# Exponentials behind a group's third copy, bf16 size matmuls, and paired weight-block copies in a two-layer attention and SwiGLU kernel

## The chip, the cores and the metric

The kernel runs on one core of a Trainium2 chip. The metric is the device time of one execution in microseconds, taken as the median of several runs. The core's engines work side by side, each through its own queue in order: TensorE (PE, matmuls, with its weight loads shown apart as PEld), VectorE (DVE), ScalarE (ACT), GpSimd (POOL), and SyncE (SP), which issues most transfers. They wait for one another through semaphores.

## The reference

The input x has 2048 tokens of 1024 features. Two equal layers follow one another; each is an attention step and a gated feed-forward step, both with a residual and a layer norm in front:

```
x = x + A_ref(layernorm(x), wqkv, wo)        # 32 heads of 32; a token sees itself and 7 earlier tokens, 2 apart
x = x + B_ref(layernorm(x), w1, w3, w2)      # (silu(x @ w1) * (x @ w3)) @ w2, with 3584 hidden features
```

Attention has only eight logits per token and head, so it isn't a matmul: the products q·k and the weighted sum over v are elementwise work. Both layers use the same weights.

## The kernel before, in words

**Units.** The tokens are cut into four chunks of 512. A unit is one chunk of one layer's feed-forward step, eight in all; units 0 to 7 are walked in order by `b_stage`. Ahead of them `q_part` computes q, k and v for layer 0; those of layer 1 follow some units later, chunk by chunk.

**Plain and seven-product matmuls.** Units 0 and 1 compute w1, w3 and w2 as plain matmuls in `b_stage` (L1279, L1288, L1310). At the same time they prepare units 2 to 7, which use a Strassen-like form (Winograd's): a matrix product cut into 2 x 2 blocks is made of seven half-size products P1 to P7 instead of eight. For this the weight blocks are needed with certain sums and differences of theirs, in fp16. `weight_size` measures a group's weights: ACT squares them into `size` (L878), a matmul with a matrix of ones adds over the partitions (L892), and DVE makes a power of two from the sum (`scale_of`). `weight_sums` copies four blocks of the group, scaled, into one of two buffers `blocks` (ACT, L910), `differences` makes four more on DVE, in part over the copied ones (L923), and POOL's queue stores seven blocks to `t_d` in memory. `sums_of_w2` does the same for w2 (L1009, L1015, stored to `t2_d`). The two buffers are used in turn, and a buffer is free again when its store has landed.

**A group.** A group is four column blocks of w1 (m = 0, the gate) or of w3 (m = 1, up); w1 and w3 alternate, and a unit has 14 groups in two splits of 8 and 6. I number them 0 to 83 over units 2 to 7. `pipeline` interleaves each group with the one before it; PE's order is P1(i), P7(i-1), P5(i), P3(i-1), P6(i), P4(i-1), P2(i), with eight 256-column matmuls each (L1052). Four results are gathered in three PSUM banks A, B and D, with three copies by ACT:

- after P1 the first copy (L1064) puts A into B, so that P2 can add to B while P6 adds to A;
- after P5 the second copy (L1069) puts D into the buffer `s5`;
- after P6 the third copy (L1073) puts A into the buffer `su`; DVE adds it to D (L1076), for P3, and P7 goes on adding to A.

After P7 DVE makes A plus `s5` (L1088, L1090), and P4 goes on in A. `consume` takes each result on: Silu on ACT for a gate (L1227), a scaled copy on ACT (L1232) and a product on DVE (L1236) for up. There are six PSUM banks for this (two more for other work), and a bank is given again in the order in which banks came free. The down projection with w2 (`W` inside `products`, L1165, copies L1173, L1181, L1185) has the same seven products, for two row blocks each.

**Attention in between.** Attention is worked off in halves of a chunk (256 tokens), 16 in all. `score_steps` multiplies q by k on DVE and folds (L590, L510 to L514), PE adds up the heads (`gather_heads`, L604), DVE takes the maximum and subtracts it (L625, L628), ACT takes the exponential (L629), DVE sums, inverts and scales (L634 to L637), POOL's queue spreads the result (L644); `value_steps` then multiplies by v (L665). The exponential and Silu need different ACT tables, so an exponential between two gates brings two table loads. When the values of a half are there, `o_tile` runs two output tiles of it on PE (L771).

**What sets the order.** The program writes every engine's order out by hand. A planner keeps an expected time for each engine in `now` and a due time for each step. `background` gives DVE the next step of several queues that fits before a time; `act_background` does so for ACT; `between` takes output tiles whose values are expected to be there. The exponential is emitted inside the DVE step that subtracts the maximum (`exps`, L627 to L630), wherever that step falls. Each step has a cost in microseconds (0.61 for a block copy, 0.40 for a difference), and changing a cost or a number of steps changes where other work is placed.

Of the kernel before, what the change touches and what calls it, by code (L numbers as in the profile page):

```python
# [7 lines left out]
FP32 = mybir.dt.float32  # L8
BF16 = mybir.dt.bfloat16
FP16 = mybir.dt.float16  # L10
I32 = mybir.dt.int32
ALU = mybir.AluOpType
# [5 lines left out]
def kernel(  # L18
# [13 lines left out]
    nc = tc.nc  # L32
# [176 lines left out]
    tight = big[:, 6144:7168].bitcast(BF16).rearrange("p (i a t) -> p i a t", i=2, a=2)  # L209
    blocks = [big[:, 3584 * i:3584 * (i + 1)].rearrange("p (b k c) -> p b k c", b=7, k=KT // 2) for i in range(2)]  # L210
    NG = NF // FG
    ones = const.tile([P, P], FP32, name="ones")
    nc.gpsimd.memset(ones[:], 1.0)
    size = const.tile([P, 2, NG, 2], FP32, name="size")
    up_scale = const.tile([P, 2, NG], FP32, name="up_scale")
# [353 lines left out]
    def pe_requests(limit=1, must=False):  # L569

        act_background()
        while pe_queue and limit and (must or pe_queue[0][0]() + 3.5 <= now["pe"]):
            pe_queue.pop(0)[1]()
            limit -= 1

    def score_steps():

        V = nc.vector
        for g, (l, h) in enumerate(halves):
# [46 lines left out]

            def exps():  # L627
                V.tensor_tensor(L[:], L[:], mx[:].unsqueeze(1).to_broadcast([P, W, BLK]), op=ALU.subtract)  # L628
                nc.scalar.activation(E[:], L[:], ACTF.Exp, scale=scale)  # L629
                at["E"] = act(0.65, now["dve"] + 0.1, "exp")  # L630

            yield 0.70, 0.0, exps
            yield 0.0, at["E"] if "E" in at else 0.0, lambda: None
            yield 0.66, at["E"], lambda: V.tensor_reduce(sm_[:], E[:].rearrange("p w e -> p e w"), op=ALU.add,  # L634
                                                         axis=AX.X)
            yield 0.56, 0.0, lambda: V.reciprocal(rs[:], sm_[:])
# [42 lines left out]
    for u in range(len(units)):  # L679
        for f0, f1 in fsplits:  # L680
            if u >= TU:
                groups = [(m, g0 // FG) for g0 in range(f0, f1, FG) for m in range(2)]
                for i, (m, g) in enumerate(groups):
                    seq += [("early", m, g)] + ([("late", *groups[i - 1])] if i else [])
                seq += [("late", *groups[-1])]
            for g0 in range(f0, f1, FG) if u < TU else ():
                seq += [(kind, g0, min(FG, f1 - g0), (u, g0 // FG) if m == u else None)
                        for m, kind in enumerate(("w1", "w3"))]
            nq = (f1 - f0) // 2
            if u >= TU:  # L690
                seq += [("t2", fsplits.index((f0, f1)), b, nq) for b in range(7)]
            else:
                seq += [("w2", g0, nq, hh) for hh in range(2) for g0 in (f0, f0 + nq)]
        if 1 <= u and u + 3 < len(units):
            seq += [("qkv", which, h) for which in range(3) for h in range(2)]
# [176 lines left out]
    def weight_size(m, g, w, at, got):  # L872

        w_ = w[:].rearrange("p k c -> p (k c)")
        half = w_.shape[1] // 2
        up, down = up_scale[:, m, g:g + 1], down_scale[:, m, g:g + 1]
        for i in range(2):
            yield 1.95, at, lambda: nc.scalar.activation(junk, w_[:, i * half:(i + 1) * half], ACTF.Square,  # L878
                                                         accum_out=size[:, m, g, i:i + 1])

        def scale_item(ps, r):
            def emit():
                opened[0] -= 1
                nc.vector.tensor_reduce(down, ps[:], op=ALU.add, axis=AX.X)
                scale_of(down, up, down)
                got["at"] = now["dve"] + 0.1
            yield 1.0, r, emit

        def add_up(t):
            ps = side_tile([P, 2], FP32, name="size", tag="sd")  # L890
            opened[0] += 1
            nc.tensor.matmul(ps[:], lhsT=ones[:], rhs=size[:, m, g, :], start=True, stop=True)  # L892
            makes.insert(0, [scale_item(ps, pe(1, t)), None])

        t = now["act"] + 2.5
        pe_queue.append((lambda: t, lambda: add_up(t)))

    def weight_sums(m, g, w, got):

        while "at" not in got:  # L900
            yield "blocked"
        KQ = KT // 2
        for a in range(2):
            while pending[a]:
                yield "blocked"
            pending[a] += 1
            b = blocks[a]
            for i, (kh, fh) in ((0, (0, 0)), (1, (0, 1)), (3, (1, 0)), (5, (1, 1))):
                c0 = fh * 256 + a * P
                yield 0.61, max(got["at"], stored[a]), lambda: nc.scalar.activation(  # L910
                    b[:, i], w[:, kh * KQ:(kh + 1) * KQ, c0:c0 + P], ACTF.Copy,
                    scale=up_scale[:, m, g:g + 1])
            makes.append([differences(m, g, a, now["act"] + 0.1), None])
        made.add((m, g))

    pending, stored, made, held = [0] * 2, [0.0] * 2, set(), []
    junk = hsum[:].bitcast(BF16).rearrange("p k t -> p (k t)")

    def differences(m, g, a, r):

        b = blocks[a]
        for out, x, y in ((4, 5, 1), (1, 1, 0), (2, 4, 0), (6, 3, 2)):
            yield 0.40, r, lambda: nc.vector.tensor_tensor(  # L923
                b[:, out], b[:, x], b[:, y], op=ALU.add if (x, y) == (4, 0) else ALU.subtract)
        pending[a] -= 1
        nc.gpsimd.dma_start(t_d[m][g][:, 4 * a:4 * (a + 1)], b[:, 0:4])
        nc.gpsimd.dma_start(t_d[m][g][:, 8 + 3 * a:8 + 3 * (a + 1)], b[:, 4:7])
        stored[a] = now["dve"] + 7.0
# [49 lines left out]
    def total_scale(sizes_, up, down, got):  # L978
# [11 lines left out]
        def add_up(t):  # L990
            ps = side_tile([P, n], FP32, name="size", tag="sd")
            opened[0] += 1
            nc.tensor.matmul(ps[:], lhsT=ones[:], rhs=sizes_[:], start=True, stop=True)
            makes.insert(0, [scale_item(ps, pe(1, t)), None])

        t = now["act"] + 2.5
# [4 lines left out]
    def sums_of_w2(i, f, ws, loaded):  # L1001
# [3 lines left out]
        a = min((i for i in range(2) if not pending[i]), key=lambda i: stored[i])  # L1005
        pending[a] += 1
        b = big[:, a * 3584:(a + 1) * 3584].rearrange("p (b c) -> p b c", b=7)
        for j, (fh, hh) in ((0, (0, 0)), (2, (0, 1)), (1, (1, 0)), (5, (1, 1))):
            yield 0.61, max(loaded, stored[a], got2["at"]), lambda: nc.scalar.activation(b[:, j], ws[hh][fh][:, f, :], ACTF.Copy,  # L1009
                                                                             scale=up2[:])  # L1010
        r = now["act"] + 0.1

        def rest():
            for out, x, y in ((4, 5, 2), (2, 2, 0), (3, 4, 0), (6, 1, 3)):
                yield 0.40, r, lambda: nc.vector.tensor_tensor(  # L1015
                b[:, out], b[:, x], b[:, y], op=ALU.add if (x, y) == (4, 0) else ALU.subtract)
            pending[a] -= 1
            nc.gpsimd.dma_start(t2_d[i][:, :, f, :], b)
            stored[a] = now["dve"] + 7.0
# [15 lines left out]
    def pipeline(key, groups, consume, done, last, fill=None):  # L1035

        xnT = xnTs[key]
        KQ = KT // 2
        sides = dict(P1=(0, xnT[:, 0:KQ, 0:HT]), P5=(1, sums[:, 0]), P6=(2, sums[:, 1]), P2=(3, xnT[:, KQ:KT, 0:HT]),
                     P7=(0, xnT[:, 0:KQ, HT:CH]), P3=(1, sums[:, 2]), P4=(2, xnT[:, KQ:KT, HT:CH]))  # L1040

        def acc():
            return psum.tile([P, 2, HT], FP32, name="st", tag="mm")
# [12 lines left out]
        def head_part(i, name):  # L1056
# [14 lines left out]
            elif name == "P6":  # L1071
                r = run(G, name, G["A"], False, G["tB"])
                nc.scalar.copy(su, G["A"][:])  # L1073
                G["tU"] = t = act(0.5, r)
                background(t + 0.8)
                nc.vector.tensor_tensor(G["D"][:], G["D"][:], su, op=ALU.add)  # L1076
                G["tD"] = dve(0.68, max(t, G["t5"])) + 0.1
# [21 lines left out]
                consume(G, 2, G["A"][:], r)  # L1099

        n = len(groups)
        for i in range(n + 1):
            for name, tail in (("P1", "P7"), ("P5", "P3"), ("P6", "P4"), ("P2", None)):
                if i < n:
                    head_part(i, name)
# [307 lines left out]
```

## Time and profile before

| what | value |
|---|---|
| median of 3 runs | 1531.82 us (1531.68 to 1533.64) |
| the profiled execution | 1532.7 us |
| its span, first to last instruction | 1531.0 us |
| PE busy | 1518.1 us (99%) |
| DVE busy | 1201.8 us (78%) |
| ACT busy | 884.1 us (58%) |
| POOL busy | 153.7 us (10%) |
| granted TensorE clock | 1.00 |

Times inside the profile count from the start of the span. In a line of the timeline the first number is the start, the second the length, then engine, line of the program, operation, output and inputs by the program's names, and in brackets how long the engine had been idle and who released it. In the view of waits a line names who waited, for whom, the microseconds in total, how often, and the longest. Table loads are a line of their own.

### The profile page before, as it was taken

Reading aid. Unit: us, or ns where it says so; the run is one execution under the profiler, and the core shown is the slowest. Engines: PE = TensorE matmul, PEld = TensorE weight load, DVE = VectorE, ACT = ScalarE, POOL = GpSimd, SP = SyncE. Lnnn points to the kernel's source line nnn. Section 1 sums busy time; section 2 is a strip of 40 time slices with the busy share of each in tenths; the row PEclk is TensorE's granted clock in tenths of the full one; section 3 lists DMA queues with packets and bytes.
Section 4 is the critical chain, followed back from the end, with each engine's and each line's share of the span. In section 5 each row is a group of like instructions: output and inputs, shape, how many; then the busy total and the mean of one; then the engine's idle time right before and its main releaser. Section 6 shows DMA issues by size and latency. Waiting matters only on the chain.

```text
span 1531.0 us, 25095 instructions
## 1 busy us (share of the span) xinstructions
PE 1518.1 (99%) x9594; PEld 989.5 (65%) x9634; DVE 1201.8 (78%) x2126; ACT 884.1 (58%) x1388; POOL 153.7 (10%) x308
## 2 busy tenths in 40 slices
PE   9999999999999999999999999999999999999999
PEld 7666644444444577575786767766677767686865
DVE  4688998889989898989698958898678986435445
ACT  3885476567665357455565564756557445554643
POOL 1210102121211101001011010100111000000000
PEclk9999999999999999999999999999999999999999
DMA  9777969798997888979779997898969988878885
GB/s 321 202 218 215 253 226 330 272 304 289 306 320 247 280 316 294 347 264 303 263 269 324 346 268 282 280 323 302 323 225 333 338 296 282 306 272 334 318 294 203
DMA packets 261432, 439.56 MB, mean 287 GB/s; under 512 B 73856, under 2 KB 201088, under 8 KB 245056
## 3 DMA queue, kind: packets, MB, share of 16 engines
q1 hardware_dynamic: 248464, 390.90, 76.8%
q0 software_dynamic: 12704, 46.93, 8.6%
q8 instruction: 75, 1.23, 0.3%
q14 instruction: 45, 0.37, 0.1%
q10 hardware_dynamic: 144, 0.13, 0.0%
HBM read 345.90 MB, written 67.90 MB: 270 GB/s over the span
## 4 chain that ended last, share of the span: by engine, by line
PE 97%; ACT 1%; issue 1%; DVE 0%; DMA 0%; SPq 0%; ACTq 0%
PE st L1052 32%; PE ps L836 21%; PE w L1165 16%; PE po L771 7%; PE pg L1279 6%; PE pu L1288 6%; PE acc L1310 6%; PE pq L444 1%; PE L L604 0%; DMA wqkv<-in_A_wqkv_dram 0%; ACT L629 0%; ACT L1227 0%; ACT E L629 0%; ACT sg L1227 0%; DVE x_sb L1150 0%
## 5 line engine op out<-in xcount | busy, mean ns | idle before, releaser
L836 PE MATMUL ps<-xnT,wqkv 128*128 128x512 f16 (+1 forms) x1469 | 320.4, 379 | 0.2
L1052 PEld LDWEIGHTS <-early 128*128 128x128 f16 x2688 | 262.6, 98 | 40.4 <-issue 3.5
L836 PEld LDWEIGHTS <-wqkv 128*128 128x128 bf16 x1472 | 210.6, 144 | 108.1 <-issue 2.2
L1165 PE MATMUL w<-t,hT 128*128 128x512 f16 x1008 | 226.0, 379 | 0.6 <-ACT big L1185 0.5
L1052 PEld LDWEIGHTS <-late 128*128 128x128 f16 x2016 | 197.2, 98 | 30.6 <-issue 2.5
L590 DVE TENSOR_TENSOR tree<-qT,kT 128x2048 bf16<-128x2048 bf16 x128 | 156.3, 1221 | 35.8 <-DMA kT<-qkv_d 18.2
L1052 PE MATMUL st<-xnT,late 128*128 128x256 f16 x1344 | 174.2, 273 | 2.2 <-ACT big L1073 2.2
L510 DVE TENSOR_TENSOR tree<-tree 128x1024 bf16<-128x1024 bf16 x256 | 175.6, 686 | 0.9
L1052 PE MATMUL st<-big,early 128*128 128x256 f16 x1344 | 172.3, 273 | 1.6 <-ACT sg L1227 1.1
L1165 PEld LDWEIGHTS <-hT 128*128 128x128 f16 x1008 | 98.2, 98 | 112.9 <-DVE hT L1136 2.0
L1052 PE MATMUL st<-xnT,early 128*128 128x256 f16 x1344 | 165.7, 273 | 0.0
L665 DVE TENSOR_TENSOR tree<-At,vT 128x2048 bf16<-128x2048 bf16 x128 | 156.2, 1221 | 11.9 <-DMA At<-E 10.7
L1064 ACT COPY st<-st 128x512 f32<-128x512 f32 x84 | 48.3, 575 | 128.1 <-PE st L1052 127.4
L771 PE MATMUL po<-wo,oT 128*128 128x512 bf16 x486 | 110.8, 379 | 1.3
L840 ACT CAST hT<-ps 128x512 bf16<-128x512 f32 x96 | 55.8, 585 | 90.6 <-PE ps L836 88.3
L1288 PE MATMUL pu<-xnT,w3t 128*128 128x512 f16 x448 | 105.8, 379 | 0.0
L1279 PE MATMUL pg<-xnT,w1t 128*128 128x512 f16 x448 | 105.8, 379 | 0.0
L1310 PE MATMUL acc<-w2t,hT 128*128 128x512 bf16 x437 | 97.8, 379 | 0.6
L1076 DVE TENSOR_TENSOR st<-st,big 128x512 f32<-128x512 f32 x84 | 58.4, 695 | 46.9 <-ACT big L1073 46.8
L1227 ACT ACTIVATE sg<-st,down_scale 128x512 bf16<-128x512 f32 x126 | 86.6, 687 | 11.6 <-PE st L1052 11.0
L1052 PE MATMUL st<-big,late 128*128 128x256 f16 x672 | 87.1, 273 | 0.0
L771 PEld LDWEIGHTS <-oT 128*128 128x128 bf16 x512 | 50.1, 98 | 55.7
(167 smaller groups left out, 1916.6 us busy)
## 6 DMA issues: line engine op xcount, KB each, us to landing
early<-t_d SPq DMA_DIRECT2D x84, 1024.0 KB, 6.9
late<-t_d SPq DMA_DIRECT2D x84, 768.0 KB, 6.2
t<-t_d SPq DMA_DIRECT2D x42, 1024.0 KB, 7.3
t<-t_d SPq DMA_DIRECT2D x42, 768.0 KB, 5.3
wqkv<-in_A_wqkv_dram SPq DMA_DIRECT2D x28, 1024.0 KB, 8.1
w1t<-in_B_w_dram SPq DMA_DIRECT2D x14, 1024.0 KB, 7.6
w3t<-in_B_w_dram SPq DMA_DIRECT2D x14, 1024.0 KB, 11.0
t_d<-big POOLq DMA_DIRECT2D x28, 512.0 KB, 6.2
```

Of the source, the lines that this page charges most:

```text
L510: nc.vector.tensor_tensor(b, b, buf[:, 4:8, :], op=ALU.add)
L590: V.tensor_tensor(pr, qT[:], kT[:, :, k0:k0 + TCH], op=ALU.mult)
L665: V.tensor_tensor(tm.rearrange("p w (a e) -> p w a e", a=4), At[:].rearrange("p a w e -> p w a e"), win, op=ALU.mult)
L771: nc.tensor.matmul(ps[:], lhsT=oT[:, t, j * P:(j + 1) * P], rhs=wo[:, t, hh * 512:(hh + 1) * 512], start=(t == 0), stop=(t == KT - 1))
L836: nc.tensor.matmul(ps[:], lhsT=ws[kk // KH][:, kk % KH, t::KT], rhs=xnT[:, kk, :], start=(kk == 0), stop=(kk == KT - 1))
L1052: nc.tensor.matmul(out[:, a, :], lhsT=w[:, a, blk, k, :], rhs=rhs[:, k, :], start=start and a == 0 and k == 0, stop=k == KQ - 1, skip_grou ...
L1076: nc.vector.tensor_tensor(G["D"][:], G["D"][:], su, op=ALU.add)
L1165: nc.tensor.matmul(out[:], lhsT=lhs[:, k, j * P:(j + 1) * P], rhs=w[:, k, :], start=start and k == 0, stop=k == nq - 1, skip_group_check=True)
L1227: nc.scalar.activation(sg[:], src, ACTF.Silu, scale=inv)
L1279: nc.tensor.matmul(pg[:], lhsT=w1t[:, kk, fi * P:(fi + 1) * P], rhs=xnT[:, kk, :], start=(kk == 0), stop=(kk == KT - 1))
L1288: nc.tensor.matmul(pu[:], lhsT=w3t[:, kk, fi * P:(fi + 1) * P], rhs=xnT[:, kk, :], start=(kk == 0), stop=(kk == KT - 1))
L1310: nc.tensor.matmul(acc[:], lhsT=hT[:, f, j * P:(j + 1) * P], rhs=tiles[hh][f // nq][:, f % nq, :], start=(f == 0), stop=(f == f1 - f0 - 1))
```

## The change

It has three parts, and a fourth that comes with them.

First, exponentials. `exps` still subtracts the maximum on DVE, but inside `pipeline` (the flag `staged`) it appends the exponential to the list `later` instead of emitting it. `run_later`, called in P6 right after the third copy, emits the first of the list if its input is expected by then. At the end of a pipeline, what is left is emitted at once. `score_steps` is blocked until its exponential has been emitted.

Second, the size matmuls. The matrix `ones` becomes bf16, and the sizes are read as the upper halves of their fp32 words.

Third, block order. The seven blocks of a buffer stand in another order, so that two copies are one ACT instruction (planned at 1.20) and two of the four differences one DVE instruction (`diff_steps`, 0.66 + 0.42 + 0.42); w2's copies stay single, its differences are paired too. Fourth, the table `sides` and the order in which t2 blocks are loaded name the new places.

```
-    ones = const.tile([P, P], FP32, name="ones")
+    ones = const.tile([P, P], BF16, name="ones")
...
+    later, staged = [], [False]
+    def run_later():
+        if later and later[0][0] <= now["act"] + 0.5:
+            later.pop(0)[1]()
...
             def exps():
                 V.tensor_tensor(L[:], L[:], mx[:].unsqueeze(1).to_broadcast([P, W, BLK]), op=ALU.subtract)
-                nc.scalar.activation(E[:], L[:], ACTF.Exp, scale=scale)
-                at["E"] = act(0.65, now["dve"] + 0.1, "exp")
+                ready = now["dve"] + 0.1
+                def exp_():
+                    nc.scalar.activation(E[:], L[:], ACTF.Exp, scale=scale)
+                    at["E"] = act(0.65, ready, "exp")
+                if staged[0]:
+                    later.append((ready, exp_))
+                else:
+                    exp_()
             yield 0.70, 0.0, exps
-            yield 0.0, at["E"] if "E" in at else 0.0, lambda: None
+            while "E" not in at:
+                yield "blocked"
+            yield 0.0, at["E"], lambda: None
...
-                seq += [("t2", fsplits.index((f0, f1)), b, nq) for b in range(7)]
+                seq += [("t2", fsplits.index((f0, f1)), b, nq) for b in (0, 2, 1, 3, 4, 6, 5)]
...
-            nc.tensor.matmul(ps[:], lhsT=ones[:], rhs=size[:, m, g, :], start=True, stop=True)
+            nc.tensor.matmul(ps[:], lhsT=ones[:], rhs=size[:, m, g, :].bitcast(BF16)[:, 1::2], start=True, stop=True)
...
-            for i, (kh, fh) in ((0, (0, 0)), (1, (0, 1)), (3, (1, 0)), (5, (1, 1))):
+            for i, j, fh in ((0, 2, 0), (3, 6, 1)):
                 c0 = fh * 256 + a * P
-                yield 0.61, max(got["at"], stored[a]), lambda: nc.scalar.activation(
-                    b[:, i], w[:, kh * KQ:(kh + 1) * KQ, c0:c0 + P], ACTF.Copy,
+                yield 1.20, max(got["at"], stored[a]), lambda: nc.scalar.activation(
+                    b[:, i:j + 1:j - i], w[:, :, c0:c0 + P].rearrange("p (h k) c -> p h k c", h=2), ACTF.Copy,
                     scale=up_scale[:, m, g:g + 1])
...
+    def diff_steps(b):
+        tt = nc.vector.tensor_tensor
+        yield 0.66, lambda: tt(b[:, 1:5:3], b[:, 3:7:3], b[:, 0:4:3], op=ALU.subtract)
+        yield 0.42, lambda: tt(b[:, 3], b[:, 4], b[:, 0], op=ALU.add)
+        yield 0.42, lambda: tt(b[:, 5], b[:, 2], b[:, 3], op=ALU.subtract)
...
-        for out, x, y in ((4, 5, 1), (1, 1, 0), (2, 4, 0), (6, 3, 2)):
-            yield 0.40, r, lambda: nc.vector.tensor_tensor(
-                b[:, out], b[:, x], b[:, y], op=ALU.add if (x, y) == (4, 0) else ALU.subtract)
+        for step in diff_steps(b):
+            yield step[0], r, step[1]
...
-            nc.tensor.matmul(ps[:], lhsT=ones[:], rhs=sizes_[:], start=True, stop=True)
+            nc.tensor.matmul(ps[:], lhsT=ones[:], rhs=sizes_[:].bitcast(BF16)[:, 1::2], start=True, stop=True)
...
-        for j, (fh, hh) in ((0, (0, 0)), (2, (0, 1)), (1, (1, 0)), (5, (1, 1))):
+        for j, (fh, hh) in ((0, (0, 0)), (3, (0, 1)), (2, (1, 0)), (6, (1, 1))):
...
-            for out, x, y in ((4, 5, 2), (2, 2, 0), (3, 4, 0), (6, 1, 3)):
-                yield 0.40, r, lambda: nc.vector.tensor_tensor(
-                b[:, out], b[:, x], b[:, y], op=ALU.add if (x, y) == (4, 0) else ALU.subtract)
+            for step in diff_steps(b):
+                yield step[0], r, step[1]
...
-        sides = dict(P1=(0, xnT[:, 0:KQ, 0:HT]), P5=(1, sums[:, 0]), P6=(2, sums[:, 1]), P2=(3, xnT[:, KQ:KT, 0:HT]),
-                     P7=(0, xnT[:, 0:KQ, HT:CH]), P3=(1, sums[:, 2]), P4=(2, xnT[:, KQ:KT, HT:CH]))
+        sides = dict(P1=(0, xnT[:, 0:KQ, 0:HT]), P5=(1, sums[:, 0]), P6=(3, sums[:, 1]), P2=(2, xnT[:, KQ:KT, 0:HT]),
+                     P7=(0, xnT[:, 0:KQ, HT:CH]), P3=(2, sums[:, 2]), P4=(1, xnT[:, KQ:KT, HT:CH]))
...
                 nc.scalar.copy(su, G["A"][:])
                 G["tU"] = t = act(0.5, r)
+                run_later()
                 background(t + 0.8)
...
+        staged[0] = True
         for i in range(n + 1):
+            if i == n:
+                staged[0] = False
+                while later:
+                    later.pop(0)[1]()
```

## The prediction

> **What bounds the kernel now.** I read the page's busy times and its chain first, then PE's own waits, then the timeline around each of them.
>
> ```profile
> PE 1518.1 (99%) x9594; PEld 989.5 (65%) x9634; DVE 1201.8 (78%) x2126; ACT 884.1 (58%) x1388; POOL 153.7 (10%) x308
> PE 97%; ACT 1%; issue 1%; DVE 0%; DMA 0%; SPq 0%; ACTq 0%
> ```
>
> TensorE sets the end from first to last. Only two things can shorten the run: less work on PE, or fewer moments in which PE waits. PE's waits are few:
>
> ```profile
> PE st L1052 <- ACT big L1073: 2.2, 1, 2.2
> PE st L1052 <- ACT sg L1227: 1.1, 1, 1.1
> PE w L1165 <- ACT big L1185: 0.5, 1, 0.5
> PE st L1052 <- ACT st L1064: 0.4, 1, 0.4
> ```
>
> The view counts from the drawn end of a matmul, and a 256-column one is drawn 273 ns long though the next starts 109 ns later. So I take as a stall what a start is later than the start before it plus 8 x 0.109 = 0.873 us for a product (0.216 us for each 512-column matmul). The waits become 2.36 us at 989.79, 1.25 at 669.13, 0.64 at 1066.02, 0.57 at 1234.06, and 0.29 at 1159.90, too short for the view: 5.11 us. All five have an exponential just before them on ACT. The one at 1234, ACT first and then PE:
>
> ```profile
> 1228.45 0.59 ACT L1073 COPY big<-st 128x512 f32<-128x512 f32 x1 [0.62 <-PE st L1052]
> 1229.06 1.28 ACT L629 ACT_TABLE_LOAD   x1
> 1230.35 0.60 ACT L629 ACTIVATE E<-L 128x512 bf16<-128x512 f32 x1
> 1230.84 0.68 ACT L1232 ACTIVATE big<-st,down_scale 128x512 bf16<-128x512 f32 x1
> 1231.54 1.28 ACT L1227 ACT_TABLE_LOAD   x1
> 1232.84 0.69 ACT L1227 ACTIVATE sg<-st,down_scale 128x512 bf16<-128x512 f32 x1
> 1233.42 0.59 ACT L1064 COPY st<-st 128x512 f32<-128x512 f32 x1
> ...
> 1232.62 1.03 PE L1052 MATMUL st<-big,late 128*128 128x256 f16 x8
> 1234.06 1.03 PE L1052 MATMUL st<-big,early 128*128 128x256 f16 x8 [0.41 <-ACT st L1064]
> ```
>
> P6 of a group accumulates into A, so it waits until the next group's first copy (L1064) has read A. From the third copy of one group to the first of the next PE has six products, 5.24 us. ACT has, start to start, 0.61 + 1.29 + 0.49 + 0.70 + 1.30 + 0.58 and the copy's 0.59, 5.56 us, and began 0.2 us after P6 ended: 0.57 us late. The largest stall has the exponential ahead of the third copy instead, which P7 needs after only three more products:
>
> ```profile
> 984.19 1.28 ACT L629 ACT_TABLE_LOAD   x1
> ...
> 989.16 0.58 ACT L1073 COPY big<-st 128x512 f32<-128x512 f32 x1
> ...
> 989.79 1.03 PE L1052 MATMUL st<-xnT,late 128*128 128x256 f16 x8 [2.19 <-ACT big L1073]
> ```
>
> The size matmuls:
>
> ```profile
> L892 PE MATMUL size<-size,ones x28: 167/210/252, 206.4 to 476.1; 128*128 128x2 f32 x28
> 311.38 1.50 PEld L1279 LDWEIGHTS <-w1t 128*128 128x128 bf16 x8
> 311.49 1.89 PE L1279 MATMUL pg<-xnT,w1t 128*128 128x512 f16 x8
> 15.68 3.74 PE L444 MATMUL pq<-xnT,wqkv 128*128 128x128 bf16 x64
> ```
>
> Fourteen of two columns and one of sixteen, each two matmul records. From the size matmul's first start (311.35) to the next start (311.49) PE loses 0.14 us in 14 cases and 0.21 in the one that a gather follows: 2.17 us. The last line is bf16 with a new weight tile every 128 columns: (3.74 - 0.22) / 63 = 0.056 us from start to start, the weight load included.
>
> **What the Trainium skill says.** "ScalarE: Activation LUTs", section "What ACT_TABLE_LOAD costs": about 1283 ns for every table, and an ACTIVATE with one pointer operand takes about 280 + 0.833 N ns, of which 93 overlap with the next. The trace agrees: 1283 ns, and a 512-wide block copy (L910) takes 711 ns, 0.612 us from start to start. "TensorE: Matmul & The Clock Gate", section "Wait — 56ns, not 53.3ns?": 55.6 and 215.7 ns for 128 and 512 columns; here 56 and 216. "FP8 and Floating Point Precision", section "TensorE Precision Notes": true FP32 takes four passes; the trace shows two records per size matmul, so I use the measured 0.14 us. "VectorE: DVE Perf Modes", section "The perf-mode tier table": tensor_tensor has a double rate for bf16 and none above; the 2048-wide row at 1221 ns is that rate.
>
> **The exponentials.** There are 16. Seven belong to the first stages, where a late gate only delays one of six PSUM banks: with two banks of 1.73 us per step a bank comes round after 10.4 us, against 1.29 + 0.60 + 1.29 us for an exponential plus one 1.04 us copy. They cost PE nothing before or after. The other nine, in order of time, with PE's stall before and after:
>
> At 587.95 it stood ahead of a third copy and cost 0, because an attention-output tile (3.45 us of PE, from 588.59) followed. It now stands right behind the third copy of group 4, in the sequence copy, table, exponential, up, table, gate, first copy, which is that of 1228.45, and in the new order no tile follows: 0.57. At 666.49, behind the third copy of an up group, the gate activation of P4 came after both tables and P5 waited for its bank: 1.25. It moves one group on, to the sequence above: 0.57. At 985.48: 2.36. It moves behind the third copy of group 34, again the same sequence; two Square passes ahead make that copy start about 0.14 us late (0.2 + 0.485 + 2 x 1.045 + 0.48 + 0.575 = 3.83 after P1, against 3.69): 0.71. At 1064.89, in the down projection: 0.64, same order after. At 1155.70: 0.29, then the same sequence, 0.57. At 1230.35: 0.57; it moves to the last group before the down projection, where P4's gate ends about 4.6 us after P6 and the bank is wanted after 4.8 us (P4, P2, P7, six matmuls, P3): 0. The other three stand among projection copies, or ahead of the s5 copies of a down projection, with over a microsecond to spare: 0. Sums: 5.11 before, 0.57 + 0.57 + 0.71 + 0.64 + 0.57 = 3.06 after; gain 2.05. DVE doesn't wait meanwhile: its sum over E is held back until the exponential is issued.
>
> **Smaller stalls.** In two down projections (878.50, 1251.06) a 1.14 us attention product between two adds held the second third copy, 0.19 + 0.11 us. In the new order a 0.33 us fold, or nothing, stands there: gain 0.3. An apply pass ahead of a third copy cost 0.16 us in group 63; one now stands so in group 21: even.
>
> **Size matmuls.** 2.17 - 15 x 0.056 - 0.09 for the entry into the gather = 1.24 us. If the next weight load isn't hidden at all (0.11 us, from 311.38 to 311.49) it is 0.45. There is one more weight load instruction each, on a PE that loads during the matmul before. I take 1.24.
>
> **Block copies and differences.** ACT: 112 copies x 0.612 = 68.5 us become 56 x 1.04 (280 + 853 - 93 ns) = 58.2. DVE: per block 4 x 0.342 become 0.602 (the pitch of 1024 elements, L510) + 2 x 0.342, over 42 blocks 3.4 us less. Both count nothing on PE, which waits for neither there. What they do is let the planner place other work earlier: attention-output tiles of the third half come at 283.4 instead of 294.3, tables and w1/w3 loads shift by a group. Loads are issued 17 to 33 us ahead of use and land in 8 to 11; the POOL stores are as many as before. If the cover were gone, each microsecond that attention values are late is one on PE. For the third half the margin is 0.2 to 1.2 us: from the seventh of eight down-projection adds on DVE has 2.0 us left, the tile is wanted 3.45 us after that sum, and the add began 1.2 us after it before (281.65 against 280.4), at best 0.2. Margins before were 1.6 to 7.6 us. The new order of the t2 blocks only names the same blocks anew.
>
> **Sum.** 2.05 + 0.3 + 1.24 = 3.6 us. The span of 1531.0 becomes 1527.4, the profiled 1532.7 becomes 1529.1. The profiled run is 0.9 us above the median of 1531.82, so the median becomes 1528.2, 0.23% less. About 0.2%, 3.1 us, is what a measurement can tell from no change; the forecast lies just past it.
>
> **Rivals.** First, no visible change: the exponential's wait is only moved. For it: four places inherit the 0.57 us that is measured at 1234, one of which had none; with one or two more stalls of 0.6 and the exposed weight load, the gain is 3.6 - 0.8 - 0.8 = 2.0: 1529.8. Second, slower: attention values late in the first two units. The double difference reads and writes with a gap; at single rate it would take about 1.2 us against 0.66 planned, 0.54 x 42 = 23 us more on a DVE that idles 43.7 us of the 418.7 from 155.4 to 574.1, and tiles would wait: about 3.4, 7 and 7.6 us over for the third to fifth half, less margins of 2 to 4, some 10 in all: 1538. It decides from 3.6 us of waits on; a milder form is a plan that runs 2 us late at three tiles, 1534. Against: inner runs are whole 512-element rows, and L590, whose eight runs of 256 are gapped too, keeps 1221 ns for 2048. Third, better: third copies start before the planner thinks and most of the 3.06 us goes as well: 1525.5.
>
> **Chances.** Forecast 0.5, no visible change 0.31, slower 0.12, better 0.07. The forecast's own range is 1527.2 to 1529.0, which crosses the 0.2% line at 1528.76, so I count a tenth of it (0.05) as no change: faster 0.45 + 0.07 = 0.52, same 0.31 + 0.05 = 0.36, slower 0.12. The range from 1526.3 to 1532.0 leaves out most of the slower case and of the better one.
>
> **What would show it.** Right: the size matmul once, and about 0.06 us to the next start; PE's waits with L1073 and the gate gone, and four or five of about 0.6 us for first copies, 5.2 us behind a third copy with an exponential; DVE's double difference near 690 ns; the double block copy near 1.13 us. Wrong: PE waiting for oT, a double difference near 1.2 us, or a third copy behind an exponential still.

## The result and the profile after

The changed kernel takes 1552.43 us (median of 4 runs, 1550.77 to 1554.37) against 1531.82 us (1531.68 to 1533.64): 1.0132 times the time before, 95% interval 1.0115 to 1.0150. The prediction was 1528.2 us, in a range from 1526.3 to 1532.0. It had the wrong sign. The profiled execution took 1551.6 us, its span is 1549.7 us (1531.0 before).

These are the busy times of the changed kernel and the shares of its chain by engine, from its page:

```profile
PE 1525.7 (98%) x9619; PEld 986.9 (64%) x9619; DVE 1198.2 (77%) x2084; ACT 874.1 (56%) x1332; POOL 162.5 (10%) x308
PE 53%; DVE 11%; DMA 5%; ACT 4%; issue 2%; POOL 0%; ACTq 0%; DVEq 0%; SPq 0%; POOLq 0%
```

ACT is 10 us less busy and DVE 3.6 us, as forecast, but the chain is on PE for 53% of the span where it was 97%: it now runs through DVE and transfers. PE's waits from 180 to 620 us, which hold the first two feed-forward units (columns as in the view of waits before: total, times, longest):

```profile
PE po L788 <- DVE down_scale L901: 4.4, 3, 2.6
PE ps L853 <- DMA wqkv<-in_A_wqkv_dram: 3.8, 1, 3.8
PE pu L1316 <- DMA w3t<-in_B_w_dram: 2.8, 1, 2.8
PE st L1074 <- DVE st L1099: 1.8, 1, 1.8
PE ps L853 <- DVE peak L1051: 1.4, 1, 1.4
```

None of the five was there before. From start to start the stalls in this stretch are 0.49 us at 214.3, 2.81 at 286.9, 1.60 at 387.4, 2.95 at 467.1, 1.59 at 524.3, 3.96 at 529.2, 1.92 at 580.0, and 0.94, 0.38, 0.28 and 0.18 elsewhere: 17.1 us, an exponential's stall apart that comes below. Behind three of them (286.9, 467.1, 529.2) the next matmuls of 512 columns start up to 0.427 us apart in place of 0.216, some eight each time: 1.46 + 1.68 + 1.52 = 4.7 us more. Together 21.8 us, where the kernel before lost 0.2. The difference is 21.6 us. Less the 1.75 us of the size matmuls and 1.2 us gained in the first stages (the first w1 matmul starts at 191.3 against 192.5), with the stalls after 620 us, that exponential's included, nearly unchanged in sum (5.7 us against 5.9), that leaves 18.7 us, which is the difference of the spans.

What the change was to do to single instructions, it did. The groups of a pair copy, the double difference and the size matmul, of the changed kernel:

```profile
L927 ACT ACTIVATE big<-w3t,up_scale 128x1024 f16<-128x1024 bf16 x28 | 31.1, 1141 | 19.2 <-DMA t_d<-big 15.5 <-DVE up_scale L887 3.7
L939 DVE TENSOR_TENSOR big<-big 128x1024 f16<-128x1024 f16 x42 | 28.8, 686 | 20.2 <-ACT big L927 10.7 <-ACT big L1032 9.5
L909 PE MATMUL size<-size,ones 128*128 128x2 bf16 x14 | 2.3, 167 | 0.0
```

The double copy takes 1141 ns (1.13 us were forecast), the double difference 686 ns (690). A size matmul is one record, and the next matmul starts 28 ns after it (282.34 and 282.37 in the next view). What has changed beside the lengths is the end of the L939 line: DVE stood 20.2 us before a difference and waited for ACT's copies, where the kernel before had 12.8 (6.3 for w1's and w3's, 6.5 for w2's).

The largest stall behind a DVE instruction, at 287 us, as the timeline of the changed kernel shows it (start, length, instruction, idle time before it and its releaser):

```profile
279.06 0.92 POOL L1040 DMA_DIRECT2D t_d<-big  x1 [11.36 <-DVE big L941]
...
282.34 0.17 PE L909 MATMUL size<-size,ones 128*128 128x2 bf16 x1
282.37 1.89 PE L788 MATMUL po<-wo,oT 128*128 128x512 bf16 x8
283.03 0.68 DVE L1352 TENSOR_TENSOR x_sb<-x_sb,acc 128x512 bf16<-128x512 bf16 x1
283.50 5.14 ACT L1032 ACTIVATE big<-w2t,up 128x512 f16<-128x512 bf16 x8 [6.41 <-DMA t_d<-big]
286.08 0.69 DVE L939 TENSOR_TENSOR big<-big 128x1024 f16<-128x1024 f16 x1 [2.38 <-ACT big L1032]
286.69 0.15 DVE L901 TENSOR_REDUCE down_scale<-size 128x1 f32<-128x2 f32 x1
...
286.90 3.78 PE L788 MATMUL po<-wo,oT 128*128 128x512 bf16 x10 [2.65 <-DVE down_scale L901]
```

ACT's copies into a block buffer wait until the store of its former content has landed. DVE's queue has the difference of those copies next, and behind it the small reduction that reads the size matmul's PSUM bank. The attention-output tile of PE needs that bank. So one late store holds ACT, DVE and PE in turn. It went out late: from its issue to ACT's start are 4.4 us, less than the 7 us that the planner allows. That ACT waits for stores is not new (37.0 us in all before, 42.5 now, summed from the lines of the copies); what stands behind these waits is. The values of the tile (oT) had been there since 282.0, as forecast.

### The profile page after: what moved, and what is told of

Read it like the earlier page. It is cut to its first block, busy times and chain, and to the rows that moved or that the text cites. A ratio compares the mean times of both kernels' runs of the same rounds, so it can differ in the third digit from the quotient of the medians.

```text
span 1549.7 us, 24962 instructions
## 1 busy us (share of the span) xinstructions
PE 1525.7 (98%) x9619; PEld 986.9 (64%) x9619; DVE 1198.2 (77%) x2084; ACT 874.1 (56%) x1332; POOL 162.5 (10%) x308
## 4 chain that ended last, share of the span: by engine, by line
PE 53%; DVE 11%; DMA 5%; ACT 4%; issue 2%; POOL 0%; ACTq 0%; DVEq 0%; SPq 0%; POOLq 0%
PE st L1074 27%; PE w L1193 15%; PE ps L853 7%; PE po L788 5%; DMA t_d<-big 3%; DVE tree L682 2%; DVE tree L510 2%; DVE tree L597 1%; DMA xnT<-xn 1%; DMA w3t<-in_B_w_dram 1%; DVE tree L512 1%; ACT sg L1255 1%; DMA kT<-qkv_d 1%; DVE hT L1320 1%; DVE big L939 1%
## 5 line engine op out<-in xcount | busy, mean ns | idle before, releaser
L788 PE MATMUL po<-wo,oT 128*128 128x512 bf16 x512 | 117.7, 382 | 5.2 <-DVE down_scale L901 4.4
```

The source lines that it names most:

```text
L788: nc.tensor.matmul(ps[:], lhsT=oT[:, t, j * P:(j + 1) * P], rhs=wo[:, t, hh * 512:(hh + 1) * 512], start=(t == 0), stop=(t == KT - 1))
```

## The experiments

Times are medians; the kernel before ran beside each group on the same chip (1532.85 us for e3 to e6, 1533.17 for e7 to e10, 1532.44 for e1, e2, e11 and e12, 1532.40 for e13, 1532.65 for e14 to e17). Times of different groups can be compared to about a microsecond, since the kernel before differs by up to that.

### Which part of the change

e3_blocks has only the pair copies, the paired differences and the new block order. e4_exps_size has only the other two parts, e1_exps only the exponentials, e2_size only the size matmuls. e5_old_costs has the whole change, but the planner is told the old steps:

```
# e5_old_costs
-                yield 1.20, max(...), lambda: nc.scalar.activation(b[:, i:j + 1:j - i], ...)
+                yield 0.61, max(...), lambda: None
+                yield 0.61, max(...), lambda: nc.scalar.activation(b[:, i:j + 1:j - i], ...)
...
-        yield 0.66, lambda: tt(b[:, 1:5:3], b[:, 3:7:3], b[:, 0:4:3], op=ALU.subtract)
-        yield 0.42, ...   (twice)
+        yield 0.40, lambda: None
+        yield 0.40, lambda: tt(b[:, 1:5:3], b[:, 3:7:3], b[:, 0:4:3], op=ALU.subtract)
+        yield 0.40, ...   (twice)
```

e6_new_plan_single is its mirror: planned as the changed kernel, but each pair is issued as two single instructions.

```
# e6_new_plan_single
-                yield 1.20, max(...), lambda: nc.scalar.activation(b[:, i:j + 1:j - i], ...)
+                yield 1.20, max(...), lambda: [nc.scalar.activation(b[:, q], w[:, kh * KQ:...], ...)
+                                               for kh, q in enumerate((i, j))]
```

> The kernel before with the block part of the change alone (paired copies and differences, new block order, new planned costs); exponentials and size matmuls as before. If the blocks make the loss (theory), it is as slow as the changed kernel without what the other two parts gain: 1552.4 + 1.7 (size) + 0 to 2 (exponentials), 1552 to 1557. If the delayed exponentials make it (rival), 1532 within 2.

> The kernel before with the exponentials and the bf16 size matmuls alone; blocks, their instructions and their planned costs as before. Theory (blocks make the loss): 1531.8 - 1.7 (15 size matmuls at 0.028 instead of 0.145 us) - 2.05 (exponential stalls 5.11 to 3.06), 1528.0, at most 1 us off. Rival (exponentials make the loss): about 1550.

> The whole change, but the planner is told the old steps and costs (two copies as two steps of 0.61, a double difference as two of 0.40), so that TensorE's order is that of the run with exponentials and size alone, with paired instructions in the places of the single ones. If the new plan makes the loss (theory A): 1528 within 1. If the paired instructions themselves make it (theory B: a gate or a difference waits for a 1.14 us copy): about 1550.

> The whole change with its new plan and TensorE's order unchanged, but each paired copy and each double difference is issued as two single instructions in the same place. Theory A (the plan makes the loss): about 1552, up to 5 more since the single ones take 10 us more of ScalarE and some 3 of VectorE. Theory B (the paired instructions make it): 1528 to 1535.

> The exponentials alone. By my sum: stalls behind exponentials 5.11 to 3.06 us, so 2.05 us less than before. If TensorE's stalls only move to other copies: within 0.7 us of before.

> The bf16 size matmuls alone, every order as before: 15 of them at 0.028 us instead of 0.14, as the changed kernel's trace has it, 1.75 us less than before; by the 0.056 us of my prediction 1.24 us less.

| run | us | against before, 95% interval |
|---|---|---|
| e3_blocks | 1553.66 | 1.0141 (1.0117 to 1.0165) |
| e4_exps_size | 1531.11 | 0.9988 (0.9979 to 0.9997) |
| e5_old_costs | 1530.39 | 0.9985 (0.9978 to 0.9992) |
| e6_new_plan_single | 1554.49 | 1.0141 (1.0126 to 1.0156) |
| e1_exps | 1530.97 | 0.9989 (0.9982 to 0.9995) |
| e2_size | 1533.35 | 1.0006 (0.9997 to 1.0015) |

The loss comes with the blocks part, and there with the plan, not with the instructions: paired instructions in the old order lose nothing, single ones in the new order lose all of it. PE's order in e5 is that of e4, in e6 that of the changed kernel. PE's waits of e6 from 180 to 620 us are the same ones, at other sizes:

```profile
PE po L788 <- DVE down_scale L901: 6.3, 3, 3.5
PE ps L853 <- DMA wqkv<-in_A_wqkv_dram: 3.8, 1, 3.8
PE pu L1317 <- DMA w3t<-in_B_w_dram: 2.1, 1, 2.1
```

The exponentials are worth 1.5 us alone. The size matmuls alone are worth nothing that can be seen, where 1.24 to 1.75 us were expected. In their trace each costs 0.028 us in place of 0.14, so the saving is there; but with PE's and DVE's order unchanged it has two stalls that the kernel before has not, 1.02 us at 561.1 behind an addition on DVE and 2.02 us at 841.1 behind a load of `late`. Only one execution was traced, so why these two came isn't shown. e4 and e5 fell short too: they gain 1.7 and 2.5 us on the kernel before beside them, where some 3.8 were expected.

### Which number of the plan

e8_old_copy_steps is the changed kernel with only the pair copy planned as two steps of 0.61 (the upper half of e5's diff). e9_old_diff_steps has only the differences planned as four steps of 0.40 (its lower half). e10_sums_new keeps the old number of steps, but the new sums: copies 2 x 0.60, differences 4 x 0.375. e12_before_costs is the kernel before with nothing changed except those two planned numbers, no instruction. e7_store10 lets the planner count on a later landing of the stores:

```
# e7_store10, in both places
-        stored[a] = now["dve"] + 7.0
+        stored[a] = now["dve"] + 10.0
```

> The whole change, with one planner constant altered: a block buffer counts as free 10 us after its differences instead of 7. Theory (the new plan counts on buffers before their stores have landed, so that differences stand at the head of VectorE's queue while ScalarE waits for a store): VectorE's waits for block copies fall from 20 us to under 10 and the time to 1528 to 1536. Rival (the plan is late for another reason): 1545 to 1560.

> The whole change, but the planner still sees a paired copy as two steps of 0.61 (the pair is issued in the second); differences planned the new way. TensorE's order is then almost that of the fast runs. If the one long copy step makes the plan late: 1528 to 1532. If the differences' new steps do: about 1550.

> The whole change, but the planner sees the differences as four steps of 0.40; the copy is one step of 1.20. If the one long copy step makes the plan late: about 1550, with 15 us or more of VectorE waiting for copies. If the differences' new steps do: 1528 to 1532.

> Paired instructions, old number of steps, but each step shortened so that the sums are the new ones: copies two steps of 0.60, differences four of 0.375. If any shift of the planned costs spoils the plan (theory of a plan that fits one set of costs): 1540 or more. If the length of one step matters and not the sum: 1528 to 1533.

> The kernel before with not one instruction changed in kind or number; only the planner's numbers are the new sums: a block copy 0.60 instead of 0.61, a difference 0.375 instead of 0.40. Theory (the plan of before fits one set of costs, and any other costs time): 1537 or more. Rival (only the paired steps spoil the plan): 1531.5 to 1534.

| run | us | against before, 95% interval |
|---|---|---|
| e7_store10 | 1636.92 | 1.0683 (1.0651 to 1.0715) |
| e8_old_copy_steps | 1529.57 | 0.9977 (0.9970 to 0.9984) |
| e9_old_diff_steps | 1531.43 | 0.9992 (0.9982 to 1.0002) |
| e10_sums_new | 1539.69 | 1.0044 (1.0024 to 1.0064) |
| e12_before_costs | 1539.97 | 1.0051 (1.0035 to 1.0067) |

Neither the new copy step alone nor the new difference steps alone spoil the plan; the two together do. A longer allowance for the stores, which ought to have mended it, makes it far worse. And e12, whose numbers are off the old ones by 0.01 and 0.025 us, loses 0.5% with no instruction changed, PE's longest new wait being one of 2.5 us for hT. e10, with the same new sums and paired instructions, loses much the same (6.5 us, e12 7.5). So small changes of these numbers move the time either way, and which way can't be read from whether a number is the truer one. e8 is the best version found, and beats both kernels: all the paired instructions, with the copies planned as before. The one wait of PE in it from 180 to 620 us:

```profile
PE po L788 <- DVE down_scale L901: 0.3, 1, 0.3
```

### Which waits make the new order late

e11_no_store_wait and e13_no_store_wait2 take the stores' landing away from the copies: the stores read the resident wo tile, which nothing overwrites then, and POOL reads one element of the block first, so that the store is still issued behind the differences.

```
+        nc.gpsimd.tensor_copy(probe[:], b[:, 5, 0, 0:2])
-        nc.gpsimd.dma_start(t_d[m][g][:, 4 * a:4 * (a + 1)], b[:, 0:4])
+        nc.gpsimd.dma_start(t_d[m][g][:, 4 * a:4 * (a + 1)], other[:, 0:4])      # other: a view of wo
```

> The whole change, every engine's order kept. The stores of the blocks read from another tile (wo), so that the transformed weights in memory are wrong, and a block copy no longer waits until the buffer's last store has landed; a tiny GpSimd copy keeps the store queue waiting for the differences as before (it may cost 0.2 us each). Theory (copies wait for stores, differences wait for copies at the head of VectorE's queue, TensorE waits for VectorE): VectorE's waits for copies fall from 20 us to under 8 and the time to 1530 to 1536. Rival (VectorE's new order is late in itself, or the weights' loads are): 1545 or more.

> As the run without store waits (stores read wo, so the transformed weights are wrong; a tiny GpSimd copy waits for the differences in the store's place), but with GpSimd's queue held to program order, which in the changed kernel it has anyway; so the stores keep their place and don't run ahead. Theory (copies wait for stores, differences wait for copies at the head of VectorE's queue, TensorE waits for VectorE): VectorE's waits for copies fall from 20 us to under 8, TensorE's waits between 200 and 620 us from 15 to under 5, time 1530 to 1538. Rival (the new order of VectorE's queue is late in itself): 1545 or more.

e11 took 1607.62 us (1.0489, 1.0468 to 1.0510) and says nothing on the question: POOL's order, alone among the engines with work here, isn't written out by hand, and with their tie to the blocks gone the stores ran ahead to between 118 and 301 us. e13 holds POOL to the order of the program. In both, the transformed weights in memory are not those of the input. e13 took 1547.02 us (1.0091, 1.0062 to 1.0121), 5.4 us less than the changed kernel, where one theory expected most of the loss back and the other nothing. PE's waits of e13 from 180 to 620 us:

```profile
PE pu L1321 <- DMA w3t<-in_B_w_dram: 4.2, 1, 4.2
PE ps L854 <- DMA wqkv<-in_A_wqkv_dram: 3.6, 1, 3.6
...
PE po L789 <- DVE down_scale L902: 0.7, 2, 0.4
```

The stalls of 2.81, 1.60 and 1.92 us at 287, 387 and 580 are down to 0.49, 0.22 and nothing. Two transfers stay, and have become the larger part. In the changed kernel the w3 load for 467 us is issued at 453.3, together with three others. ACT's queue ahead of them:

```profile
436.25 2.56 ACT L1032 ACTIVATE big<-w2t,up 128x512 f16<-128x512 bf16 x4
444.95 1.91 ACT L895 ACTIVATE hsum<-w3t 128x2048 bf16<-128x2048 bf16 x1 [6.14 <-DMA w3t<-in_B_w_dram]
...
446.99 1.91 ACT L895 ACTIVATE hsum<-w3t 128x2048 bf16<-128x2048 bf16 x1
...
448.89 4.99 ACT L1032 ACTIVATE big<-w2t,up 128x512 f16<-128x512 bf16 x8
```

and SP's queue, before and after:

```profile
435.97 0.37 SPq L727 DMA_DIRECT2D w1t<-in_B_w_dram  x1
439.09 0.37 SPq L727 DMA_DIRECT2D w3t<-in_B_w_dram  x1
443.17 0.37 SPq L727 DMA_DIRECT2D w1t<-in_B_w_dram  x1
444.93 1.87 SPq L727 DMA_DIRECT2D w3t<-in_B_w_dram  x1
```

```profile
452.07 0.37 SPq L744 DMA_DIRECT2D w1t<-in_B_w_dram  x1
453.30 0.37 SPq L744 DMA_DIRECT2D w3t<-in_B_w_dram  x1
453.76 1.02 SPq L744 DMA_DIRECT2D w1t<-in_B_w_dram  x1
454.88 7.80 SPq L744 DMA_DIRECT2D w3t<-in_B_w_dram  x1
```

The last eight w2 copies stand behind a size pass (L895) that waits for a weight tile on its way. They are the last readers of the w2 tiles, and SP may not overwrite those earlier: four loads go out within 3 us, and this one 13.7 us ahead of the matmul at 467.05, which had to wait for its landing. Before, the copies and size passes alternated, the loads went out one by one from 436, and the same one went out at 439.1, 21.3 us ahead of its use at 460.4.

Four more runs were made on this. e14_sizes_ready is e13 with the size passes reading the resident wo tile; e17_sizes_ready_stores has that alone, with the stores' wait left in. e15_wqkv_queue is the changed kernel with the projection weights of the later units loaded from ACT's queue, where no transpose stands ahead of them; e16_both is e14 with that. In e14, e16 and e17 the sizes and the stored weights are not those of the input.

```
# e14, e17
-        w_ = w[:].rearrange("p k c -> p (k c)")
+        w_ = wo[:].rearrange("p t d -> p (t d)")[:, 0:4096]
# e15, e16
-                nc.sync.dma_start(w[:, k0:k0 + step, :], wqkv_v...)
+                (nc.sync if len(w_tiles) < 6 else nc.scalar).dma_start(w[:, k0:k0 + step, :], wqkv_v...)
```

> e13 (stores that don't hold the block copies back) with one more wait away: the size passes read the resident wo tile in place of the weight tile that is still on its way, so ScalarE does not stand before a size pass while block copies are queued behind it. The sizes and the stored weights are therefore wrong; the instructions and their order on TensorE, VectorE and ScalarE are those of e13. Loads held up by block copies: the last eight w2 copies of the first down projection finish near 439 us in place of 451.8, the four loads behind them go out near 440, and TensorE's wait for the w3 tile at 464 (4.39 us, and 13 matmuls at half rate, 2.6 us) is gone: 1547.0 - 7.0 = 1540. VectorE's new order late in itself: nothing changes, 1547.

> The changed kernel whole, with one difference: the projection weights of the later units are loaded from ScalarE's queue, at the same place in the program, in place of SyncE's, where they stand behind the transposes of the normalised input. Loads behind transposes: the first goes out near 509.5 us in place of 515.1, TensorE's wait for it at 529.5 (3.96 us, and eight matmuls at half rate, 1.70 us) is gone, and 1552.4 becomes 1546.8. If the transposes and the loads only share the transfer engines, the wait stays within 1 us of what it was: 1551.5 to 1552.5.

> e14 and e15 together: no wait of the copies for stores, none of the size passes for loads (sizes and stored weights wrong), projection weights from ScalarE's queue. If these three waits are the loss: 1547.0 - 7.0 - 6.2 = 1533.8, that is 1.001 of the kernel before. If VectorE's new order is late in itself: 1541 or more.

> The changed kernel, only the size passes reading the resident wo tile (sizes wrong, and so the stored weights), the copies waiting for the stores as they did. If the stores hold the same copies back just as long, the two stores before them go out at 438.0 and 442.5 us and land some 7 us later, so the last copies still end near 452, the w3 load is as late as before, and the time stays at 1551 to 1552.5. If the size pass alone holds the copies, the wait at 467 (2.95 and 1.68 us) goes and 1547.8 is left.

| run | us | against before, 95% interval |
|---|---|---|
| e14_sizes_ready | 1539.81 | 1.0043 (1.0028 to 1.0058) |
| e15_wqkv_queue | 1554.30 | 1.0137 (1.0122 to 1.0152) |
| e16_both | 1549.39 | 1.0106 (1.0088 to 1.0124) |
| e17_sizes_ready_stores | 1546.88 | 1.0091 (1.0074 to 1.0109) |

e14 came out at the 1540 expected of late loads. Its ACT queue and its SP queue:

```profile
432.08 1.90 ACT L896 ACTIVATE hsum<-wo 128x2048 bf16<-128x2048 bf16 x1
...
434.10 1.91 ACT L896 ACTIVATE hsum<-wo 128x2048 bf16<-128x2048 bf16 x1
...
436.01 5.00 ACT L1036 ACTIVATE big<-w2t,up 128x512 f16<-128x512 bf16 x8
```

```profile
439.19 0.37 SPq L745 DMA_DIRECT2D w1t<-in_B_w_dram  x1
440.42 0.37 SPq L745 DMA_DIRECT2D w3t<-in_B_w_dram  x1
```

The copies end at 441.0, the w3 load goes out at 440.4, and the stall at 464 (4.39 us, and 13 slow matmuls) is gone: 7.2 us, the whole difference between the two runs. DVE's order is the same in both, so it is not the order of DVE in itself that made this part. e17's time is within 1 us of the second of its expectations (1547.8), but not for the reason given there: the copies still waited for stores and went at 444.4 and 448.8, and the w3 load went out at 450.7, 2.6 us sooner. That was enough to leave 0.98 us of the stall and none of its slow matmuls. With either wait gone 5.4 or 5.5 us come back, with both 12.6, so the two are worth about as much together as one by one. Not all of e17's gain is the size passes' own: its reduction at 287 still holds PE for 2.81 us, but no slow matmuls follow, which is 1.5 us in this trace.

e14 has 6.8 us of stalls left at the projections that follow the second unit: 1.30 us at 513.9, 3.72 at 518.6 for the weights, and 1.74 in slow matmuls. Its distance to the kernel before is 7.2 us. SP's queue at this place, of the kernel before and then of e14:

```profile
486.77 4.14 SPq L707 DMA_DIRECT2D wqkv<-in_A_wqkv_dram  x2
506.05 12.03 SPq L272 DMA_TRANSPOSE xnT<-xn  x4
518.18 2.69 SPq L707 DMA_DIRECT2D wqkv<-in_A_wqkv_dram  x4
```

```profile
500.08 5.00 SPq L273 DMA_TRANSPOSE xnT<-xn  x2
505.14 2.04 SPq L725 DMA_DIRECT2D wqkv<-in_A_wqkv_dram  x2
508.19 10.58 SPq L273 DMA_TRANSPOSE xnT<-xn  x2
518.87 2.72 SPq L725 DMA_DIRECT2D wqkv<-in_A_wqkv_dram  x4
```

Before, the first two projection loads stood ahead of all four transposes of the normalised input. In the new order they stand behind two of them, go out 18 us later (in the changed kernel at 515.1), and meet the transposes with all 16 transfer engines taken (a share of 1.00 from 500 to 520 us, 0.73 before). e15 and e16 removed that stall, at 529.2 and at 518.6, and put a longer one in its place, 9.19 us at 546.1 and 14.09 at 541.4. PE's and DVE's longest waits in e16 from 495 to 550 us, and the loads on ACT's queue:

```profile
PE L L612 <- DVE psm L515: 13.9, 1, 13.9
DVE big L299 <- DMA xnT<-xn: 13.8, 1, 13.8
```

```profile
493.34 0.94 ACTq L725 DMA_DIRECT2D wqkv<-in_A_wqkv_dram  x2
502.12 16.65 ACTq L725 DMA_DIRECT2D wqkv<-in_A_wqkv_dram  x4
```

The scores wait for DVE, and DVE for the transposes, which are now the late ones. But these two runs moved all six projection loads. The first two left at 493.3 in e16, so their tiles were free by then, and the projections began at 513.5 without a stall; the other four left from 502.1 on, among the transposes, where in e14 they left at 518.9, behind them. Against the kernel before only the first two have changed their place in the order. To move these two alone was not tried, so it stays open whether an earlier place for them closes the last 7 us.

## Why the prediction was wrong

**The step that failed** is that of the block copies and differences: "Both count nothing on PE, which waits for neither there. What they do is let the planner place other work earlier". The first sentence holds for the instructions (e5: 0.9985). The second names the right effect, and I gave it no price. The new placement costs PE 21.8 us. By the runs 12.6 us of the loss come from two waits of ACT's copies, for the landing of stores and behind a size pass that waits for a load (5.4 for the first taken alone, 7.2 for the second after it, each to about a microsecond, since these are times of different groups). About 7 us are left, which the trace puts at two projection loads that stand behind transposes in SP's queue; that share is read, not shown by a run, and why the two new planned numbers together, and neither alone, bring this order about stays open.

**The cover that I named was the old plan's.** I counted that loads go out 17 to 33 us ahead and land in 8 to 11. The landings are about the medians of the page (7.6 us for w1, 11.0 for w3); single w1 and w3 loads of the trace before took 5.4 to 18.1 us, and the cover was still 10 us at the least. In the changed kernel the w3 load went out 13.7 us ahead of its use at 467 and took all of that to land; in that stretch w3 loads took between 13.7 and 17.9 us. I checked one margin, that of the third half's values, and it held: they were there at 282.0. What was late a moment later was the PSUM bank behind a size reduction in the same DVE queue. The new plan moves a weight tile's last readers, and I did not follow from it to the tile's release and to the load on SP's queue, though the order of the instructions was there to read.

**The rivals.** The slower one, with 0.12, was right on the side and on the place, the first two units, and its point of decision (3.6 us of waits) was far exceeded. Its cause was wrong: the double difference ran at 686 ns. Its milder form, a plan 2 us late at three tiles, was nearest, but it too stopped at the attention values.

**The exponentials** were forecast to leave 3.06 us of stalls in five places. The changed kernel shows 0.575, 0.573, 0.745, 0.633 and 0.576 us, 3.10 in all. The one at 1179, from its timeline:

```profile
1174.14 1.28 ACT L639 ACT_TABLE_LOAD   x1
1175.43 0.60 ACT L639 ACTIVATE E<-L 128x512 bf16<-128x512 f32 x1
...
1176.63 1.28 ACT L1255 ACT_TABLE_LOAD   x1
...
1178.51 0.59 ACT L1086 COPY st<-st 128x512 f32<-128x512 f32 x1
...
1179.15 1.03 PE L1074 MATMUL st<-big,early 128*128 128x256 f16 x8 [0.41 <-ACT st L1086]
```

Both table loads and the exponential stand ahead of the first copy, as worked out. Alone, the part gained 1.5 us of the 2.05.

**The size matmuls** were put at 0.056 us each and cost 0.028, so the term is 1.75 us, not 1.24. The nearest row, bf16 with a weight load every 128 columns, priced the 128 columns and not the load, which the matmul of 512 columns ahead covers whole.

**Smaller stalls** were to fall by 0.3 us. In their place eight of 0.2 to 0.5 us stand after 620 us, 2.6 us in all against 0.8 before. Seven of them, 2.4 us, stand in e1 too, which has the exponentials alone: so that part brings them, and they take back much of what it gains.

**The sum's method.** With all or some of the old numbers in the planner (e5, e8) the whole change gains 2.5 and 3.6 us. 3.6 is what I forecast, but that e8 hits it is in part luck. In its trace the exponentials' stalls are four and come to 2.5 us (forecast 3.06 in five), the size matmuls gain 1.7 (forecast 1.24), and the smaller stalls grow by about 1.6, where they were to fall by 0.3: errors of both signs. And the sum counts on an order that stays as it was, which the changed kernel's doesn't.

## What to carry to other kernels

When a planner with due times places the work, a new cost or a new number of steps is a new program: price it by following every tile whose last reader moves, to its release, to the load or store behind that and to the queue it stands in, and not by the changed instructions. Feed the planner the old numbers first (e5 does, e8 for the copies): that parts the instructions' own worth from the order's. Where a plan depends on its numbers this closely (0.5% for 0.01 and 0.025 us), truer numbers are no reason to expect a better one.

## What the hardware showed that was not expected

**Matmuls after a wait.** After a wait of PE the next matmuls of 512 columns may start 0.427 us apart in place of 0.216. The Trainium skill, "TensorE: Matmul & The Clock Gate", section "What's actually happening", has the clock halved after an idle window of about 3.4 us which runs free of the program, and restored after as long a busy one. The halved rate agrees, and the slow stretches of 3.2 to 3.6 us in the changed kernel do too; in e13 one lasted 5.8 us, after a wait of 4.39. The threshold doesn't: waits of 2.81 and 2.95 us were enough in the changed kernel, where 1.60 and 1.92 us did nothing. 2.81 us at the same place in e17 did nothing either, which a free-running window would explain. Over all runs no length parts the two cases: 2.24 us were enough in e6 (at 468), 2.97 us did nothing in e17 (at 573). A wait followed by slow matmuls cost 1.5 to 1.7 us above its length in the changed kernel, in e13 2.8 and 2.3; I had counted waits at their length.

**A two-column bf16 matmul** costs 28 ns in a stream of 512-column ones (from its start at 282.34 to the next), its weight load and the next one's included; in fp32 it cost 140 ns.
